# Attention over eight heads at a time: key and value windows of 128 columns, one buffer each

## The chip, the core and the metric

The kernel runs on one core of one Trainium2 chip. The core has five engines that run their own instruction streams and wait for each other by semaphores: TensorE (PE, with the loading of weights shown apart as PEld), VectorE (DVE), ScalarE (ACT), GpSimd (POOL) and SyncE (SP), which here issues nearly all the DMAs. The metric is the time of one launch on the device, in microseconds; lower is better. All arithmetic is done in 32 bits; a product is made of three TensorE passes over a high part and a low part of each operand.

## The reference

One transformer block on x of 2048 positions by 512 columns. A layer norm, then attention with 32 heads of 16 columns in which every position looks at 8 positions only: itself and the ones 2, 4, ... 14 before it. Then the output product and the residual; then a second layer norm and an MLP of width 1792 with a squared ReLU, again with a residual.

```python
qkv = transpose((layernorm(x) @ wqkv).reshape(B, S, 3, H, Dh))   # H = 32, Dh = 16
idx = pos[:, None] - arange(8)[None, :] * 2                      # positions before 0 are masked
logits = einsum("bhsd,bhswd->bhsw", q, k[idx]) * Dh ** -0.5
o = einsum("bhsw,bhswd->bhsd", softmax(logits), v[idx])
h = x + o @ wo
r = max(layernorm(h) @ w1 + b1, 0)
out = h + (r * r) @ w2 + b2
```

## The kernel before, in words

The 16 row tiles of 128 positions are taken in a permuted order, so that the positions a head looks at lie in one partition. The work has these stages. First the queries, keys and values of the first four tiles, one fourth of the columns at a time (products of 384 columns, `qkv`); then those of the other twelve tiles (`first_phase`, products of 512 columns). Each result leaves PSUM by ScalarE (`evac`) and goes to a scratch tensor in DRAM, `qkv_d`, laid out by groups of `GC` columns (`store`). After that come three rounds `u` of the MLP on four tiles each, with two products per slot, `mlp1` (line 228) and `mlp2` (line 900), and a last round with fewer multiplications (`products_a`, `products_b`, line 823).

Attention runs on VectorE and GpSimd beside these products, from about 25 us on. It is a Python generator, `attention()`. It goes over items: an item is a stretch `s` of 2 positions per partition, and `ng` groups of `GH` heads (`G` = 8 groups of 4 heads, `GC` = 64 columns). For each group of an item there is

- a load of a window of keys (`load_k`) and one of values (`load_v`) from `qkv_d` into SBUF, and for two groups together one of queries (`load_q`), all issued on SP; ScalarE copies the queries to PSUM (`q_to_psum`, line 268);
- on VectorE `dots` (line 340: queries times keys, 1024 elements a partition, into a tile `pr`), a reduction over the 16 columns of a head (line 374), and one item later `weigh` (line 351: weights times values, again into a `pr`);
- on GpSimd `add_up` (line 408), three halving additions over the window into `o`.

The softmax between (lines 363 to 393, and an exponential on ScalarE, line 397) is done for a whole item at once. The tiles `k` and `v` have two buffers each, `pr` has three for both uses.

The order of instructions on each engine is fixed when the program is built. `end_slot(pe)` closes a slot of TensorE's work; it adds the slot's planned length to `now["pe"]`, runs the chores that were put down for the slot, and calls `pump()`, which takes steps from the generator until the planned time of VectorE, `now["dve"]`, has reached that of TensorE. Each `yield` names the planned cost of a step; `SLOW` multiplies it. `o_T` and `o_split` call `pump(until=s)`, which takes steps until a stretch's `o` is complete. Each engine then executes its list in order; SP too, so a load that waits for its buffer holds up the DMAs behind it.

Scratch rows of 2 KB (`row()`, a pool of `ROWS` = 15 buffers) serve many names: `xt`, `xh`, `xl`, `h`, `hn`, `oh`, `ol`, `r`, `rl`. The high part `rh` of the hidden rows has a pool of its own, of four.

VectorE also makes what TensorE waits for: the low parts `xl` and `ol` of transposed operands (line 155), the residual `h` (line 666), the low parts of the MLP's input in `big_l`.

Of the kernel before, what the change touches and what calls it, by code (L numbers as in the profile page):

```python
# [16 lines left out]
P = 128  # L17
# [5 lines left out]
G = 8  # L23
# [6 lines left out]
ROWS = 15  # L30
LAG = 3
HALF = 2.6
# [26 lines left out]
def block_kernel(ctx, tc, x, wqkv, wo, w1, b1, w2, b2, out):  # L59
# [196 lines left out]
    def load_q(n, j):  # L256
        s, g0, ng = items[n]
        u, b, e, i0 = where(s)
        q = att.tile([P, 2, RI, GC], F32, name="q")
        nc.sync.dma_start(q.rearrange("p j i c -> p j (i c)"),  # L260
                          chain(e, g0 + j, 0, PAD + CH // 2 * b + i0,
                                [[R * GC, P], [CS, 2], [1, RI * GC]]))
        return q

    def q_to_psum(q):
        qp = psum.tile([P, D], F32, name="qp", tag="qp")[:, :2 * RI * GC].rearrange(
            "p (j i c) -> p j i c", j=2, i=RI)
        nc.scalar.copy(qp, q)  # L268
        return qp

    def attention():
# [3 lines left out]
        def ready(n):  # L275
            gps = [(items[n][1] + j) // 2 for j in range(0, items[n][2], 2)] if n < N else []
# [13 lines left out]
        def load_k(n, j):  # L290
            if ready(n) and (n, j) not in ks:
                ks[n, j] = ks[n - 1, j] if items[n][0] == 1 else load_window(n, j, 1, "k")
                if j % 2 == 0:
                    qs[n, j] = load_q(n, j)
# [11 lines left out]
        for j in range(2):  # L306
            load_k(0, j)
        for j in range(2):
            load_v(0, j)
        for _ in range(DELAY):  # L310
            yield None
        for n in range(N + 1):
# [5 lines left out]
            if new:  # L318
# [3 lines left out]
                for j in range(2):  # L322
                    load_k(n, j)
# [11 lines left out]
            def dots(j):  # L335
                kwin = window(ks[n, j], s, [1, GC])
                pr = att.tile([P, RI, W, GH, DH], F32, name="pr", bufs=3)
                if j % 2 == 0:
                    qps["now"] = qps.pop((n, j))
                nc.vector.tensor_tensor(  # L340
                    out=pr.rearrange("p i w h d -> p i w (h d)"),
                    in0=qps["now"][:, j % 2].unsqueeze(2).to_broadcast([P, RI, W, GC]),
                    in1=kwin, op=ALU.mult)
                load_k(*ahead(n, j, 2))
                return pr

            def weigh(j):
                load_v(n - 1, j)
                vwin = window(vs[n - 1, j], s1, [DH, GH], [1, DH])
                p2 = att.tile([P, RI, W, GH, DH], F32, name="pr", bufs=3)  # L350
# [5 lines left out]
                load_v(*ahead(n - 1, j, 2))  # L356

            for j in range(max(ng, ng1)):
                if j < ng:
                    pr = dots(j)  # L360
                    yield 1.22
                if old and j == 0:
                    nc.vector.tensor_reduce(out=sm, in_=e1.rearrange("p i w h -> p i h w"),
                                            axis=X, op=ALU.add)
                    yield 0.23 + 0.035 * ng1
                if 0 < j < ng1 or 0 < j == ng1 < ng:
                    if j == 1:
                        nc.vector.tensor_tensor(
                            out=e1, in0=e1, op=ALU.mult,
# [889 lines left out]
```

## Time and profile before

| what | us |
|---|---|
| median of 3 runs (504.65 to 506.39) | 505.88 |
| the profiled execution, first to last instruction | 501.7 |
| TensorE busy | 496.2 (99%) |
| weight loads busy | 421.2 (84%) |
| VectorE busy | 382.9 (76%) |
| ScalarE busy | 298.3 (59%) |
| GpSimd busy | 356.2 (71%) |
| share of TensorE in the chain that ended last | 98% |
| data moved by DMA | 102.61 MB, mean 205 GB/s |

The span is the profiled execution from its first to its last instruction; the times of the runs lie about 4 us above it, since a run also holds what is before and after. TensorE's busy time has to be read with care, as its instructions overlap in the records; how often a new one starts says more. The granted clock of TensorE was 1.000 throughout.

### The profile page before, as it was taken

What the parts mean: (1) busy time and instruction counts of PE and PEld (TensorE: products, weight loads), DVE (VectorE), ACT (ScalarE), POOL (GpSimd) and SP (SyncE); (2) the same over time, 40 slices, a digit from 0 to 9 for tenths busy, and PEclk for the clock granted to TensorE, in tenths of its full rate; (3) what the DMA queues carried; (4) which work ended last, traced back from release to release, by engine and by line L of the source; (5) the groups of instructions that cost most, each with busy time, mean ns of one, the idle gap of its engine ahead of it and who ended that gap; (6) DMA issues with size and microseconds to landing.
All of it is one profiled execution on the core that took longest, in us unless ns stands there. A gap on an engine that the chain in (4) does not pass through costs nothing.

```text
span 501.7 us, 7533 instructions
## 1 busy us (share of the span) xinstructions
PE 496.2 (99%) x2422; PEld 421.2 (84%) x2422; DVE 382.9 (76%) x520; ACT 298.3 (59%) x538; POOL 356.2 (71%) x434
## 2 busy tenths in 40 slices
PE   8999999999999999999999999999999999999997
PEld 7999888888888888888888888888888888998986
DVE  6479899988989989788879998888975147833223
ACT  4635777668346758378564555755555837666551
POOL 5714898886685999969777877769799464775610
PEclk9999999999999999999999999999999999999999
DMA  9668979989698989679577756967665472354112
GB/s 275 202 205 243 300 237 312 270 273 275 212 223 256 299 277 260 205 216 237 190 254 209 215 146 192 237 209 242 210 159 115 112 197 84 137 161 143 64 43 84
DMA packets 109359, 102.61 MB, mean 205 GB/s; under 512 B 29448, under 2 KB 77832, under 8 KB 109320
## 3 DMA queue, kind: packets, MB, share of 16 engines
q1 hardware_dynamic: 108376, 101.61, 69.5%
q10 hardware_dynamic: 944, 0.52, 0.3%
q8 instruction: 19, 0.31, 0.3%
q14 instruction: 20, 0.16, 0.1%
HBM read 72.65 MB, written 24.25 MB: 193 GB/s over the span
## 4 chain that ended last, share of the span: by engine, by line
PE 98%; DMA 1%; ACT 0%; ACTq 0%; DVE 0%; issue 0%
PE mm L228 49%; PE acc L900 30%; PE wo L228 9%; PE mm L823 7%; PE tr L201 2%; DMA wraw<-in_A_wqkv_dram 1%; PE half L923 0%; ACTq L562 0%; ACT big_h L152 0%; ACT xh L152 0%; PE tr L730 0%; DVE h L925 0%
## 5 line engine op out<-in xcount | busy, mean ns | idle before, releaser
L408 POOL TENSOR_TENSOR pr<-pr 128x512 f32<-128x512 f32 (+1 forms) x128 | 133.9, 1046 | 35.1 <-DVE pr L351 29.7
L228 PE MATMUL mm<-big_l,w_h 128*128 128x512 f32 x336 | 88.4, 389 | 0.0
L351 DVE TENSOR_TENSOR pr<-ex,v 128x1024 f32<-128x1024 f32 x64 | 78.0, 1220 | 12.7 <-POOL o L408 9.8
L340 DVE TENSOR_TENSOR pr<-qp,k 128x1024 f32<-128x1024 f32 x64 | 76.8, 1200 | 11.1 <-ACT qp L268 7.6
L374 DVE TENSOR_REDUCE ex<-pr 128x64 f32<-128x1024 f32 x64 | 78.5, 1226 | 2.0
L228 PEld LDWEIGHTS mm<-big_l,w_h 128*128 128x128 f32 x336 | 63.0, 188 | 13.2 <-issue 0.2
L155 POOL TENSOR_TENSOR rl<-r,rh 128x512 fp32r<-128x512 f32 x42 | 55.2, 1317 | 22.3 <-ACT rh L152 22.2
L228 PE MATMUL mm<-big_l,xh 128*128 128x512 f32 (+1 forms) x208 | 55.8, 378 | 0.0
L228 PE MATMUL mm<-big_h,xh 128*128 128x512 f32 (+1 forms) x208 | 53.6, 379 | 0.8 <-ACT xh L152 0.8
L228 PE MATMUL mm<-big_h,xl 128*128 128x512 f32 (+1 forms) x208 | 52.7, 375 | 0.0
L900 PE MATMUL acc<-big_l,rh 128*128 128x512 f32 x190 | 52.2, 390 | 0.0
L900 PE MATMUL acc<-big_h,rh 128*128 128x512 f32 x190 | 52.1, 391 | 0.0
L900 PE MATMUL acc<-big_h,rl 128*128 128x512 f32 x190 | 51.7, 389 | 0.0
L228 PE MATMUL mm<-big_l,w_l 128*128 128x512 f32 x168 | 44.9, 389 | 0.0
L228 PEld LDWEIGHTS mm<-big_h,xh 128*128 128x128 f32 x208 | 37.7, 188 | 7.7 <-ACT xh L152 1.9
L228 PEld LDWEIGHTS mm<-big_h,xl 128*128 128x128 f32 x208 | 38.2, 188 | 6.1 <-DVE xl L155 0.3
L900 PEld LDWEIGHTS acc<-big_h,rl 128*128 128x128 f32 x190 | 35.7, 188 | 7.4
L900 PEld LDWEIGHTS acc<-big_l,rh 128*128 128x128 f32 x190 | 35.5, 188 | 7.4
L228 PEld LDWEIGHTS mm<-big_l,xh 128*128 128x128 f32 x208 | 37.5, 188 | 4.9
L900 PEld LDWEIGHTS acc<-big_h,rh 128*128 128x128 f32 x190 | 34.9, 188 | 6.7
L876 ACT ACTIVATE r<-mm,b_sb 128x512 f32<-128x512 f32 x42 | 28.8, 685 | 18.9 <-PE mm L228 18.1
L228 PEld LDWEIGHTS mm<-big_l,w_l 128*128 128x128 f32 x168 | 31.5, 188 | 6.6
(163 smaller groups left out, 912.3 us busy)
## 6 DMA issues: line engine op xcount, KB each, us to landing
k<-qkv_d SPq DMA_DIRECT2D x48, 288.0 KB, 3.5
v<-qkv_d SPq DMA_DIRECT2D x48, 288.0 KB, 3.9
qkv_d<-y SPq DMA_DIRECT2D x18, 512.0 KB, 4.1
big_l<-w2l_d SPq DMA_DIRECT2D x24, 256.0 KB, 2.6
xt<-in_A_x_dram SPq DMA_DIRECT2D x16, 256.0 KB, 4.1
q<-qkv_d SPq DMA_DIRECT2D x32, 128.0 KB, 3.1
h<-in_A_x_dram SPq DMA_DIRECT2D x16, 256.0 KB, 3.8
h_d<-h SPq DMA_DIRECT2D x16, 256.0 KB, 2.5
```

Source lines behind the costliest of these rows:

```text
L155: eng.tensor_tensor(out=dst, in0=src, in1=h, op=ALU.subtract)
L201: nc.tensor.transpose(tr[:, k, :], src[:, k * P:(k + 1) * P], ident)
L228: nc.tensor.matmul(ps, l(k), r(k), start=(n == 0), stop=(n == 3 * KB - 1))
L340: nc.vector.tensor_tensor(out=pr.rearrange("p i w h d -> p i w (h d)"), in0=qps["now"][:, j % 2].unsqueeze(2).to_broadcast([P, RI, W, GC]) ...
L351: nc.vector.tensor_tensor(out=p2, in1=vwin, op=ALU.mult, in0=e1[:, :, :, j * GH:(j + 1) * GH].unsqueeze(4).to_broadcast([P, RI, W, GH, DH]))
L374: nc.vector.tensor_reduce(out=lf[:, :, :, j * GH:(j + 1) * GH], in_=pr, axis=X, op=ALU.add)
L408: nc.gpsimd.tensor_tensor(out=dst, in0=p2[:, :, :w], in1=p2[:, :, w:2 * w], op=ALU.add)
L823: nc.tensor.matmul(ps, sta[y][:, k], mov[x][:, k], start=(first and q == 0), stop=(last and q == len(terms) - 1), skip_group_check=True)
L876: nc.scalar.activation(r, ps, AF.Relu, bias=b1_sb[:, f:f + 1])
L900: nc.tensor.matmul(acc[j], l[:, j * P:(j + 1) * P], w[f], start=(first and n < len(js)), stop=(last and n >= len(terms) - len(js)))
```

## The change

Groups become twice as wide and half as many: `G` = 4 groups of 8 heads, 128 columns. So every `dots`, its reduction and every `weigh` take 2048 elements a partition instead of 1024, and the product tile `pr` has 8 KB instead of 4 KB. An item holds the same heads as before, in 1 or 2 groups instead of 2 or 4. In detail:

- `k` and `v` windows are twice as large (4608 bytes a partition instead of 2304, and 5632 instead of 2816 in the first stretches) and have one buffer each. A load is asked for one group ahead instead of two.
- `pr` becomes two tiles of one buffer each: `pr0` for `dots`, `pr1` for `weigh`.
- Queries are loaded and copied to PSUM for one group at a time, which has the columns of two before: as many loads and copies as before.
- In the loop over an item's groups, `weigh(j)` now follows `dots(j)` at once, where before `weigh(j - 1)` did; the reciprocal moves to the sum before it.
- Stores to `qkv_d` have pieces of 1024 bytes instead of 512, and the stores of the first four tiles need one DMA instead of two.
- `rh` comes from the shared rows, of which there are 17 instead of 15 plus 4.
- The planner's costs are written anew; `pump()` stops 0.8 us (`LEAD`) before TensorE's planned time, and `HALF` grows from 2.6 to 4.6.
- Two normalisations and two transposes of `x` in the first stage come one slot earlier.
- Raw weights at the start, and the combined weights of the last round, find their place in the new `pr` tiles.

```diff
-G = 8
+G = 4
 GH = H // G
 GC = GH * DH
...
-ROWS = 15
+ROWS = 17
 LAG = 3
-HALF = 2.6
+HALF = 4.6
+LEAD = 0.8
...
-    items = [(s, g0, 2) for g0 in range(0, G, 2) for s in range(RI)]
-    items += [(s, g0, 4) for s in range(RI, NS) for g0 in range(0, G, 4)]
+    items = [(s, g0, 1) for g0 in range(G) for s in range(RI)]
+    items += [(s, g0, 2) for s in range(RI, NS) for g0 in range(0, G, 2)]
...
-        t = att.tile([P, R + W - 1, GC], F32, name=name)
+        t = att.tile([P, R + W - 1, GC], F32, name=name, bufs=1)
...
-        q = att.tile([P, 2, RI, GC], F32, name="q")
-        nc.sync.dma_start(q.rearrange("p j i c -> p j (i c)"),
+        q = att.tile([P, RI, GC], F32, name="q")
+        nc.sync.dma_start(q.rearrange("p i c -> p (i c)"),
                           chain(e, g0 + j, 0, PAD + CH // 2 * b + i0,
-                                [[R * GC, P], [CS, 2], [1, RI * GC]]))
+                                [[R * GC, P], [1, RI * GC]]))
...
             def dots(j):
                 kwin = window(ks[n, j], s, [1, GC])
-                pr = att.tile([P, RI, W, GH, DH], F32, name="pr", bufs=3)
-                if j % 2 == 0:
-                    qps["now"] = qps.pop((n, j))
+                pr = att.tile([P, RI, W, GH, DH], F32, name="pr", tag="pr0", bufs=1)
...
-                load_k(*ahead(n, j, 2))
+                load_k(*ahead(n, j, 1))
...
             def weigh(j):
                 load_v(n - 1, j)
                 vwin = window(vs[n - 1, j], s1, [DH, GH], [1, DH])
-                p2 = att.tile([P, RI, W, GH, DH], F32, name="pr", bufs=3)
+                p2 = att.tile([P, RI, W, GH, DH], F32, name="pr", tag="pr1", bufs=1)
...
-                load_v(*ahead(n - 1, j, 2))
+                load_v(*ahead(n - 1, j, 1))
 
             for j in range(max(ng, ng1)):
                 if j < ng:
                     pr = dots(j)
-                    yield 1.22
+                    yield 2.29
                 if old and j == 0:
                     nc.vector.tensor_reduce(out=sm, in_=e1.rearrange("p i w h -> p i h w"),
                                             axis=X, op=ALU.add)
-                    yield 0.23 + 0.035 * ng1
-                if 0 < j < ng1 or 0 < j == ng1 < ng:
-                    if j == 1:
-                        nc.vector.tensor_tensor(
-                            out=e1, in0=e1, op=ALU.mult,
-                            in1=sm.unsqueeze(2).to_broadcast([P, RI, W, ng1 * GH]))
-                    weigh(j - 1)
-                    yield 1.55 if j == 1 else 1.26
+                    nc.vector.reciprocal(sm, sm)
+                    yield 0.5 + 0.07 * ng1
+                    nc.vector.tensor_tensor(
+                        out=e1, in0=e1, op=ALU.mult,
+                        in1=sm.unsqueeze(2).to_broadcast([P, RI, W, ng1 * GH]))
+                if j < ng1:
+                    weigh(j)
+                    yield 2.63 if j == 0 else 2.33
...
-        while (done[until] < G) if until is not None else (now["dve"] < now["pe"]):
+        while (done[until] < G) if until is not None else (now["dve"] < now["pe"] - LEAD):
...
-            for j in range(2):
-                nc.sync.dma_start(chain(e, 2 * gp + j, 0, pos,
-                                        [[R * GC, P], [G * CS, 3], [1, RI * GC]]), y[:, :, j])
+            nc.sync.dma_start(chain(e, gp, 0, pos,
+                                    [[R * GC, P], [G * CS, 3], [1, RI * GC]]), y)
...
-        rh, rl = work.tile([P, D], F32R, name="rh", bufs=LAG + 1), row("rl", dt=F32R)
+        rh, rl = row("rh", dt=F32R), row("rl", dt=F32R)
...
-        if n in (11, 12):
-            at(0, x_norm, n - 7)
-        if n in (13, 14):
-            x_T(n - 9)
+        if n in (10, 11):
+            at(0, x_norm, n - 6)
+        if n in (12, 13):
+            x_T(n - 8)
```

The change moves instructions. First VectorE in the first round of the MLP, at the start of an item of 16 heads (`pr<-qp,k` is `dots`, `ex<-pr` its reduction, `pr<-ex,v` is `weigh`, `sm` and `ex,sm` are the softmax's scaling). Before:

```order
L340 TENSOR_TENSOR pr<-qp,k 128x1024
L363 TENSOR_REDUCE sm<-ex 128x32
L374 TENSOR_REDUCE ex<-pr 128x16x4
L380 RECIPROCAL sm<-sm 128x32
L340 TENSOR_TENSOR pr<-qp,k 128x1024
L368 TENSOR_TENSOR ex<-ex,sm 128x256
L351 TENSOR_TENSOR pr<-ex,v 128x1024
L374 TENSOR_REDUCE ex<-pr 128x16x4
```

And now, at the start of such an item:

```order
L335 TENSOR_TENSOR pr<-qp,k 128x2048
L358 TENSOR_REDUCE sm<-ex 128x32
L360 RECIPROCAL sm<-sm 128x32
L362 TENSOR_TENSOR ex<-ex,sm 128x256
L346 TENSOR_TENSOR pr<-ex,v 128x2048
L369 TENSOR_REDUCE ex<-pr 128x16x8
L335 TENSOR_TENSOR pr<-qp,k 128x2048
L346 TENSOR_TENSOR pr<-ex,v 128x2048
```

Between two `dots` there are now always a `weigh` and a reduction, and in the first pair of an item the three instructions of the softmax's scaling; the second load of keys into the one buffer falls into that stretch.

Next VectorE where the first stage of `first_phase` needs the low parts `xl` of the transposed tiles 6 and 7. Before:

```order
L340 TENSOR_TENSOR pr<-qp,k 128x1024
L368 TENSOR_TENSOR ex<-ex,sm 128x128
L351 TENSOR_TENSOR pr<-ex,v 128x1024
L374 TENSOR_REDUCE ex<-pr 128x16x4
L155 TENSOR_TENSOR xl<-tr,xh 128x512
L383 TENSOR_TENSOR ex<-ex,mask 128x128
L351 TENSOR_TENSOR pr<-ex,v 128x1024
L155 TENSOR_TENSOR xl<-tr,xh 128x512
```

And now:

```order
L335 TENSOR_TENSOR pr<-qp,k 128x2048
L358 TENSOR_REDUCE sm<-ex 128x16
L360 RECIPROCAL sm<-sm 128x16
L362 TENSOR_TENSOR ex<-ex,sm 128x128
L346 TENSOR_TENSOR pr<-ex,v 128x2048
L369 TENSOR_REDUCE ex<-pr 128x128
L156 TENSOR_TENSOR xl<-tr,xh 128x512
L374 TENSOR_TENSOR ex<-ex,mask 128x128
L379 TENSOR_REDUCE mx<-ex 128x16
L381 TENSOR_TENSOR ex<-ex,mx 128x128
L156 TENSOR_TENSOR xl<-tr,xh 128x512
```

In the program up to the first of these two `xl` there stand 8 `dots`, 8 reductions and 5 `weigh` before, and 4, 4 and 3 of double length now; the second `xl` no longer has a `weigh` in front of it.

Last TensorE, at the end of the stage with products of 384 columns, where the transposes of `x` stand a slot earlier. Before:

```order
L228 MATMUL mm<-big_l,xh 128x384 x4
L228 MATMUL mm<-big_h,xh 128x384 x4
L228 MATMUL mm<-big_l,xh 128x384 x4
L228 MATMUL mm<-big_h,xl 128x384 x4
L201 MATMUL tr<-ident,xt 128x128 x4
L228 MATMUL mm<-big_h,xh 128x384 x4
```

And now:

```order
L229 MATMUL mm<-big_l,xh 128x384 x4
L202 MATMUL tr<-ident,xt 128x128 x4
L229 MATMUL mm<-big_h,xh 128x384 x4
L229 MATMUL mm<-big_l,xh 128x384 x4
L229 MATMUL mm<-big_h,xl 128x384 x4
L202 MATMUL tr<-ident,xt 128x128 x4
```

One block of four transposes has moved ahead by one product. Otherwise TensorE's list has the same instructions in the same order as before.

More of the change, by code (lines that the diff above doesn't have):

```diff
@@ L275, in ready @@
         def ready(n):
-            gps = [(items[n][1] + j) // 2 for j in range(0, items[n][2], 2)] if n < N else []
+            gps = [items[n][1] + j for j in range(items[n][2])] if n < N else []
             return n < N and all((items[n][0] // RI, gp) in stored and gp in padded
@@ L511, in store @@
             elif c == 2:
[L512 removed]
+                stored.update((t // R, gp) for gp in range(G))
     ys = {}
```

61 lines of the change are left out of this document (27 added, 34 removed).

## The prediction

> **What bounds the kernel now.** I read the page first: span, busy times, and the chain that ended last.
>
> ```profile
> span 501.7 us, 7533 instructions
> PE 496.2 (99%) x2422; PEld 421.2 (84%) x2422; DVE 382.9 (76%) x520; ACT 298.3 (59%) x538; POOL 356.2 (71%) x434
> PE 98%; DMA 1%; ACT 0%; ACTq 0%; DVE 0%; issue 0%
> ```
>
> The chain runs through TensorE for 98% of the span. A busy TensorE can still be a waiting one, so next I asked for its waits in the whole trace, and for the busy times in windows of 20 us.
>
> ```profile
> PE tr L952 <- POOL ident masks.py:199: 1.3, 1, 1.3
> PE mm L228 <- ACT xh L152: 0.8, 1, 0.8
> ```
>
> ```profile
> 0.00:20.00 20.00, 17.87 (x96) 15.97 (x97) 13.29 (x21) 11.52 (x24) 14.29 (x27) 1.00 0.82 245
> 160.00:180.00 20.00, 20.00 (x89) 16.53 (x89) 18.26 (x22) 11.70 (x21) 17.29 (x17) 1.00 0.84 267
> 380.00:400.00 20.00, 20.00 (x90) 16.53 (x89) 5.70 (x9) 15.13 (x20) 13.10 (x18) 1.00 0.37 91
> ...
> 6.83 1.27 PE L228 MATMUL mm<-big_h,xh 128*128 128x384 f32 x4 [0.78 <-ACT xh L152]
> ```
>
> Two waits, 2.1 us together; the later one ends at 6.83, as the last row says. The columns are PE, PEld, DVE, ACT and POOL with instructions in brackets. TensorE does 89 products in 20 us while VectorE is busy for 18.26 us and GpSimd for 17.29, and 90 while VectorE is busy for 5.70. So its pace does not hang on how full the others are. The pieces of the chain say the same:
>
> ```profile
> 171.34 2.72 PE acc L900 x12
> 190.38 2.72 PE mm L228 x12
> ```
>
> Twelve products of 512 columns take 2.72 us, 227 ns each, in both kinds of product. TensorE issues without a gap from about 7 us to the end; what the other engines do is hidden unless it comes too late for TensorE.
>
> **The change, part by part.** TensorE's own list changes by one block of transposes that stands a slot earlier: **0**. All other terms are on engines under cover, so I price what they save, and then whether any of them gets later than TensorE allows. From the view that groups instructions by line and shape:
>
> ```profile
> L408 POOL TENSOR_TENSOR pr<-pr 128x512 f32<-128x512 f32 x64 | 83.8, 1309 | 30.1 <-DVE pr L351 29.7
> L374 DVE TENSOR_REDUCE ex<-pr 128x64 f32<-128x1024 f32 x64 | 78.5, 1226 | 2.0
> L351 DVE TENSOR_TENSOR pr<-ex,v 128x1024 f32<-128x1024 f32 x64 | 78.0, 1220 | 12.7 <-POOL o L408 9.8 <-POOL pr L408 0.6
> L340 DVE TENSOR_TENSOR pr<-qp,k 128x1024 f32<-128x1024 f32 x64 | 76.8, 1200 | 11.1 <-ACT qp L268 7.6 <-POOL o L408 3.4
> L408 POOL TENSOR_TENSOR pr<-pr 128x256 f32<-128x256 f32 x64 | 50.1, 783 | 5.0
> L408 POOL TENSOR_TENSOR o<-pr 128x128 f32<-128x128 f32 x64 | 30.1, 471 | 5.0
> L368 DVE TENSOR_TENSOR ex<-ex,sm 128x256 f32<-128x256 f32 x12 | 5.1, 421 | 0.0
> L391 DVE TENSOR_REDUCE mx<-ex 128x32 f32<-128x256 f32 x12 | 5.0, 413 | 0.0
> L268 ACT COPY qp<-q 128x256 f32<-128x256 f32 x32 | 12.0, 375 | 25.3 <-DMA q<-qkv_d 16.0 <-DVE pr L340 8.4 <-DVE ex L368 0.9
> ```
>
> *VectorE.* No row shows 2048 elements. Between 256 and 1024 a product grows by (1220 - 421) / 768 = 1.04 ns an element, a reduction by (1226 - 413) / 768 = 1.06. Another 1024 elements make 2.27 us for `dots`, 2.29 for `weigh`, 2.31 for the reduction: 6.87 us where two narrow groups took 7.29. Times 32 that is **13.5 us less work**. The bounds are no saving (twice the row) and 13.5; I take the second, since the slope is measured on the same operations.
>
> *GpSimd.* From 256 to 512 elements an addition grows by (1309 - 783) / 256 = 2.05 ns an element, so 1024 take 2.36 us (at most 2.62, twice the row). An `add_up` then is 2.36 + 1.31 + 0.78 = 4.45 us against 2 x 2.56 = 5.13: 32 times 0.68, **22 us less work**.
>
> Neither shows in the time, as nothing on the chain waited for them. And the planner does not leave the saving idle: it keeps VectorE level with TensorE's planned time, so attention runs ahead and ends earlier; the cover of the small urgent instructions does not grow by itself.
>
> *Where they could be late.* (1) **Keys and queries.** The next keys may be loaded only when `dots` has read the one buffer, and must be there when the next `dots` starts. Inside an item the scaling of the softmax, a `weigh` and a reduction lie between.
>
> ```profile
> L363 DVE TENSOR_REDUCE sm<-ex 128x32 f32<-128x256 f32 x12 | 4.9, 411 | 0.4 <-ACT ex L397 0.4
> 217.21 0.34 DVE L380 RECIPROCAL sm<-sm 128x32 f32<-128x32 f32 x1
> L247 SPq DMA_DIRECT2D k<-qkv_d x56: 319/320/843, 21.0 to 357.6; - x56
> k<-qkv_d SPq DMA_DIRECT2D x48, 288.0 KB, 3.5
> v<-qkv_d SPq DMA_DIRECT2D x48, 288.0 KB, 3.9
> q<-qkv_d SPq DMA_DIRECT2D x32, 128.0 KB, 3.1
> ```
>
> The window is 0.41 + 0.34 + 0.42 + 2.29 + 2.31 = 5.8 us. A load of 288 KB lands 3.5 us after its issue. The other 288 KB cost at least nothing and at most the same again (7.0). I take what moves 295 KB at the 267 GB/s of the window quoted: 1.1 us, so 4.6. Behind it the queries are issued some 0.4 us later (a key load holds SP 0.32 us, the median in the row), and ScalarE needs 0.38 us to copy them: 5.4 us. It fits by 0.4. Between items the maximum and the subtraction (0.4 us each) take the scaling's place, or stand beside it. (2) **Values**: from one `weigh` to the next of an item lie 2.31 + 2.27 = 4.6 us; a load lands after 3.9, or 5.0 with the 1.1: late by 0.4 in 12 places at most, where no chore fills the gap. (3) **GpSimd's sum** must have emptied `pr1` in the same 4.6 us: 4.45 fits, but one `rl` (1.3 us) ahead of it does not. VectorE waited 9.8 + 3.4 us for these sums and 7.6 for queries already; I put the new waits, 12 times 0.4 and about 12 times 1.2, against those 20.8 us and count **0** more. SP has 56 window loads to issue instead of 112.
>
> (4) **The rows.** `rh` now takes a third row per hidden block, so a row comes round sooner: 17 / 3 against 15 / 2 blocks, still beyond the three slots that `rh` and `rl` live. I count 0; a row that is freed late would hold ScalarE before `r`, and with it a bank that TensorE needs.
>
> (5) **Long instructions ahead of urgent ones.** The tightest places are these, where TensorE starts on a low part just after VectorE has written it:
>
> ```profile
> 60.86 1.23 DVE L374 TENSOR_REDUCE ex<-pr 128x64 f32<-128x1024 f32 x1
> 62.00 0.68 DVE L155 TENSOR_TENSOR xl<-tr,xh 128x512 fp32r<-128x512 f32 x1
> 62.73 1.19 PE L228 MATMUL mm<-big_h,xl 128*128 128x512 f32 x4
> ...
> 236.78 1.21 DVE L155 TENSOR_TENSOR ol<-pl,oh 128x512 fp32r<-128x512 f32 x1
> 238.50 1.07 PE L228 MATMUL wo<-wo_h,ol 128*128 128x512 f32 x4
> ```
>
> The `xl` ends at 62.68, 0.05 us before its use; the `ol` at 237.99, 0.51 before. Ahead of that `xl` there stand 21 attention instructions (8, 8 and 5) at 1.2 us, 25.5 us; now 11 (4, 4 and 3), 9.16 + 9.24 + 6.87 = 25.3. So it comes 0.2 us earlier, if VectorE waits no longer than the 1.7 us it waited before:
>
> ```profile
> 55.39 1.22 DVE L340 TENSOR_TENSOR pr<-qp,k 128x1024 f32<-128x1024 f32 x1 [1.68 <-POOL o L408]
> ```
>
> There the sum has 4.6 us plus some 1.9 of softmax, since an item is one group in that stage; 4.45 fits, and the wait should go. I count 0 to 2 us of gain in slack, nothing in time.
>
> (6) **The end of `o`.** ScalarE waited for the last sum of a stretch, and all it did later was late by that:
>
> ```profile
> 217.80 1.05 ACT L621 COPY pl<-o 128x1024 uint16<-128x1024 uint16 x1 [2.08 <-POOL o L408]
> ```
>
> Now `weigh` follows `dots` without the lag of a group, so `o` is whole earlier. A gain in slack again.
>
> The sum: 501.7 + 0 = 501.7 us, and the run's time lies 505.88 - 501.7 = 4.2 above the span: **505.9 us, no change**.
>
> **The rivals.** *A. The buffers bind* (slower). The place is the second `dots` of the 12 items with two groups, the price is how much keys, queries or the sum overrun their window. At 7.0 us for the keys the overrun is 2.0 us; at 1.0 it is 12 us over three rounds. VectorE can make up only where it idles for TensorE:
>
> ```profile
> 204.02 0.69 DVE L666 TENSOR_TENSOR h<-wo,h 128x512 f32<-128x512 f32 x1 [1.50 <-PE wo L228]
> 212.18 0.69 DVE L666 TENSOR_TENSOR h<-wo,h 128x512 f32<-128x512 f32 x1 [1.21 <-PE wo L228]
> ```
>
> With 2.7 us there and the 0.5 of slack before `ol` in each of three rounds, some 8 us would reach TensorE: 514. It decides from an overrun of about 0.35 us on. For it: VectorE is busy 18.26 of 20 us, and SP holds loads back behind others. Against: chores stand in many of the windows. [...]
>
> *B. An urgent instruction behind a long one* (slower). A miss at a place like the two of (5) costs up to one long instruction, 2.3 us, 1.2 on average; TensorE then is later against VectorE and the next places are safe. Two misses: 508.3. For it: slack of 0.05 and 0.51. Against: the counts above, and `LEAD`, which holds attention back by 0.8 us.
>
> *C. The rows bind* (slower): ScalarE held once per round for the 1.3 us of an `rl`: 3.9 us, 509.8. Against: the count in (4).
>
> *D. Faster.* TensorE may have room that its records hide, and the 13.5 us come through: 492. Against it stand 89 and 90 products in the two windows. Short of that, the start has 20.00 - 17.87 = 2.1 us of gaps, of which fewer and larger DMAs could win a part: 504.3. [...]
>
> **How the numbers follow.** Chances: forecast 0.60, A 0.13, B 0.19, C 0.04, D 0.04. A difference under 0.3% (1.5 us) cannot be told from none here. The forecast is no change; A, B and C are slower; D is faster: 0.04, 0.60, 0.36. The forecast's own range is 504.7 to 507.2, the spread of the runs and a stall of an us. The range for 8 in 10 reaches down to D's short form and takes in B and C and the cheaper half of A: 504.3 to 511.
>
> **What would show it.** Attention's last product of before:
>
> ```profile
> 378.84 1.23 DVE L351 TENSOR_TENSOR pr<-ex,v 128x1024 f32<-128x1024 f32 x1 [0.60 <-POOL pr L408]
> ```
>
> Right: TensorE's two waits stay the only ones; `dots` and `weigh` at 2.27 and 2.29 us, the wide sum at 2.4; attention ending earlier than these 380 us; no wait of ScalarE for `o` near 217 us. For A: waits of `dots` for `qp` or of `weigh` for a load or a sum, of over 0.4 us, in most items, followed by TensorE waiting for `ol` or for `big_l`. For B: one or two waits of TensorE for `xl` or `ol` of 1 to 2 us. For C: `r` or `rh` waiting on TensorE or GpSimd. The prediction is wrong if TensorE shows over 1.5 us of new waits, or a product takes other than 227 ns.

## The result, and the profile after

The changed kernel takes 526.38 us (median of 4 runs, 524.65 to 527.94), the kernel before 506.13 on the same chip. The ratio is 1.042, 95% interval 1.0395 to 1.0446: some 20 us slower, where no change was forecast and 511 was the end of the range. The profiled execution took 524.82 us, 1.8 us above its span. From the changed kernel's page:

```profile
span 523.0 us, 7203 instructions
PE 503.3 (96%) x2422; PEld 424.5 (81%) x2422; DVE 385.5 (74%) x424; ACT 299.0 (57%) x538; POOL 339.6 (65%) x338
PE 27%; DVE 4%; DMA 3%; ACT 2%; issue 2%; POOL 2%; SPq 0%; ACTq 0%; POOLq 0%; DVEq 0%
```

The chain that ended last is no longer TensorE's alone. Its waits in the whole trace (us in total, times, longest), which were two of 2.1 us together:

```profile
PE mm L229 <- DVE big_l L156: 8.2, 2, 5.1
PE tr L202 <- ACT hn L197: 2.1, 1, 2.1
PE tr L202 <- DVE ol L156: 1.6, 1, 1.6
PE wo L229 <- DVE ol L156: 1.5, 2, 1.0
PE tr L944 <- POOL ident masks.py:199: 1.3, 1, 1.3
PE mm L229 <- ACT xh L153: 0.7, 1, 0.7
PE tr L718 <- ACT hn L197: 0.6, 1, 0.6
```

The windows of 20 us show a second loss. After the TensorE columns the granted clock is the number behind POOL's:

```profile
160.00:180.00 20.00, 14.58 (x56) 11.61 (x56) 17.31 (x18) 11.33 (x25) 10.06 (x8) 0.83 0.61 209
260.00:280.00 20.00, 18.14 (x68) 14.80 (x69) 17.77 (x20) 8.65 (x15) 10.69 (x8) 0.83 0.50 169
```

56 products where there were 89, and a clock of 0.83 where it was 1.00. TensorE's list is almost the same in both kernels, so I set the start of each product beside its start before. It gets late in these places only (`y` is a result on its way to DRAM, `hn` the normalised `h`):

| start in the changed kernel (us) | late against before, from then on (us) | what TensorE waited for |
|---|---|---|
| 124.85, transposes of `x` | 1.5 | VectorE's `ol` |
| 160.41, transposes of `hn` | 2.0 | ScalarE's `y` |
| 167.56, first product of the MLP | 7.3, and 9.5 some 5 us later | VectorE's `big_l`; then products at half speed |
| 248.46, output product | 10.0 | VectorE's `ol` |
| 261.86, second round of the MLP | 13.4, and 16.2 some 6 us later | VectorE's `big_l`; then products at half speed |
| 343.88, output product | 17.4 | VectorE's `ol` |
| 354.46, transposes of `hn` | 19.8 | ScalarE's `hn` |
| 440.54 and 448.38, last round | 20.6, 21.2 | `hn`, `wo_l` |

**The long waits.** What VectorE, GpSimd and TensorE did at the first of them, from the timelines of the three engines:

```profile
160.69 6.06 DVE L156 TENSOR_TENSOR big_l<-pl,big_l 128x256 fp32r<-128x256 f32 x4 [1.74 <-ACT big_l L153]
...
160.41 3.79 POOL L396 TENSOR_TENSOR pr<-pr 128x1024 f32<-128x1024 f32 x2
164.29 0.78 POOL L396 TENSOR_TENSOR o<-pr 128x256 f32<-128x256 f32 x1
165.03 1.44 POOL L156 TENSOR_TENSOR big_l<-raw,big_h 128x512 fp32r<-128x512 f32 x1
...
161.36 1.09 PE L229 MATMUL mm<-big_h,xl 128*128 128x512 f32 x4
167.56 2.04 PE L229 MATMUL mm<-big_l,w_h 128*128 128x512 f32 x4 [5.11 <-DVE big_l L156]
169.40 1.91 PE L229 MATMUL mm<-big_l,w_l 128*128 128x512 f32 x4
```

Four subtractions of 256 columns, the low parts of the MLP's input, take 6.06 us, while GpSimd goes through a sum and one subtraction of its own. And behind the wait four products of 512 columns take 1.91 us, 427 ns from one to the next instead of 227. Before the change the same four took 2.94 us, and the product behind them came without a wait:

```profile
155.64 2.94 DVE L155 TENSOR_TENSOR big_l<-pl,big_l 128x256 fp32r<-128x256 f32 x4 [0.65 <-ACT big_l L152]
158.50 0.74 DVE L155 TENSOR_TENSOR big_l<-tr,big_l 128x256 fp32r<-128x256 f32 x2
...
160.28 1.09 PE L228 MATMUL mm<-big_l,w_h 128*128 128x512 f32 x4
```

The form of the operand tells why. `pl` lies in SBUF (a tile turned by DMA), `tr` in PSUM (turned by TensorE). In the groups by line and shape, of before:

```profile
L155 DVE TENSOR_TENSOR big_l<-pl,big_l 128x256 fp32r<-128x256 f32 x16 | 10.2, 694 | 2.8 <-ACT big_l L152 2.8
L155 DVE TENSOR_TENSOR big_l<-tr,big_l 128x256 fp32r<-128x256 f32 x14 | 5.2, 412 | 1.1 <-PE acc L900 0.9 <-ACT big_l L152 0.2
```

and of the changed kernel, with the rows of attention itself:

```profile
L156 DVE TENSOR_TENSOR big_l<-pl,big_l 128x256 fp32r<-128x256 f32 x16 | 17.7, 1165 | 4.8 <-ACT big_l L153 4.8
L156 DVE TENSOR_TENSOR big_l<-tr,big_l 128x256 fp32r<-128x256 f32 x14 | 5.0, 408 | 0.0
L335 DVE TENSOR_TENSOR pr<-qp,k 128x2048 f32<-128x2048 f32 x32 | 73.1, 2284 | 16.2 <-ACT qp L269 13.6 <-DMA v<-qkv_d 1.8
L346 DVE TENSOR_TENSOR pr<-ex,v 128x2048 f32<-128x2048 f32 x32 | 73.3, 2289 | 11.9 <-POOL o L396 9.7 <-DMA v<-qkv_d 0.5
L369 DVE TENSOR_REDUCE ex<-pr 128x128 f32<-128x2048 f32 x32 | 73.2, 2287 | 0.6
L396 POOL TENSOR_TENSOR pr<-pr 128x1024 f32<-128x1024 f32 x32 | 77.9, 2435 | 24.9 <-DVE pr L346 24.9
L396 POOL TENSOR_TENSOR pr<-pr 128x512 f32<-128x512 f32 x32 | 42.5, 1327 | 2.5
L396 POOL TENSOR_TENSOR o<-pr 128x256 f32<-128x256 f32 x32 | 23.8, 743 | 2.5
```

The same subtraction takes 412 ns with one operand in PSUM, and 694 and now 1165 ns in the mean with both in SBUF. Theory **P**: such a subtraction is held until GpSimd's running instruction ends, and the next one by GpSimd's next instruction (the four at 160.69 us end at 163.08, 164.49, 165.35 and 166.75, each 0.28 us after an instruction of GpSimd), so a sum with an addition of 2.4 us in it holds four in a row for 6 us.

**The short waits.** Theory **Queue**: a load of keys or values into its buffer stands at the head of SP's in-order queue until VectorE has read the buffer, and what stands behind (queries, the transposes by DMA) comes late. SP's waits at the loads, before:

```profile
SPq L247 <- DVE pr L351: 45.6, 33, 3.5
SPq L247 <- DVE pr L340: 38.9, 23, 3.6
SPq L247 <- DVE mx L391: 22.3, 12, 2.9
SPq L247 <- DVE sm L363: 16.6, 10, 3.0
SPq L247 <- DVE ex L368: 16.5, 10, 2.6
```

and now:

```profile
SPq L248 <- DVE pr L346: 59.6, 25, 5.9
SPq L248 <- DVE sm L358: 46.2, 12, 6.5
SPq L248 <- DVE pr L335: 44.4, 12, 7.0
```

In the sum it is little more, 150 against 140 us; but 49 pieces of up to 7.0 us have taken the place of 88 of up to 3.6. Followed back in the trace, the wait of TensorE at 124.85 leads to a load of queries behind a load of keys: `dots` waited 1.4 us for them, and the `ol` that TensorE needed stood behind it. The waits at 343.88 and 354.46 lead to a transpose of `o` that SP issued at 332.7, behind such a load (330.96) and another transpose. On the way from there, the `ol` stood behind a late `dots` of 2.3 us (340.94), and the `hn` waited for a normalisation that stood in GpSimd's list behind the sum of a late `weigh` and an `rl`, until 352.2 us. The wait at 248.46 fits P: its `ol<-pl,oh` took 2.13 us beside an addition, the one at 343.14 only 0.68.

### The profile page after: what moved, and what is told of

Its sections match the earlier page's. It is cut to its first block, busy times and chain, and to the rows that moved or that the text cites. A ratio compares the mean times of both kernels' runs of the same rounds, so it can differ in the third digit from the quotient of the medians.

```text
span 523.0 us, 7203 instructions
## 1 busy us (share of the span) xinstructions
PE 503.3 (96%) x2422; PEld 424.5 (81%) x2422; DVE 385.5 (74%) x424; ACT 299.0 (57%) x538; POOL 339.6 (65%) x338
## 5 line engine op out<-in xcount | busy, mean ns | idle before, releaser
L396 POOL TENSOR_TENSOR pr<-pr 128x1024 f32<-128x1024 f32 x64 | 120.4, 1881 | 27.5 <-DVE pr L346 24.9
L229 PE MATMUL mm<-big_l,w_h 128*128 128x512 f32 x336 | 92.0, 401 | 8.2 <-DVE big_l L156 8.2
L335 DVE TENSOR_TENSOR pr<-qp,k 128x2048 f32<-128x2048 f32 x32 | 73.1, 2284 | 16.2 <-ACT qp L269 13.6
L229 PEld LDWEIGHTS mm<-big_l,w_h 128*128 128x128 f32 x336 | 65.4, 195 | 22.8 <-issue 9.0
L346 DVE TENSOR_TENSOR pr<-ex,v 128x2048 f32<-128x2048 f32 x32 | 73.3, 2289 | 11.9 <-POOL o L396 9.7
L369 DVE TENSOR_REDUCE ex<-pr 128x128 f32<-128x2048 f32 x32 | 73.2, 2287 | 0.6
L229 PE MATMUL mm<-big_l,w_l 128*128 128x512 f32 x168 | 46.6, 400 | 0.0
L229 PEld LDWEIGHTS mm<-big_l,w_l 128*128 128x128 f32 x168 | 32.7, 195 | 7.0
```

What stands on the lines that cost most here:

```text
L229: nc.tensor.matmul(ps, l(k), r(k), start=(n == 0), stop=(n == 3 * KB - 1))
L335: nc.vector.tensor_tensor(out=pr.rearrange("p i w h d -> p i w (h d)"), in0=qps.pop((n, j)).unsqueeze(2).to_broadcast([P, RI, W, GC]), in1 ...
L346: nc.vector.tensor_tensor(out=p2, in1=vwin, op=ALU.mult, in0=e1[:, :, :, j * GH:(j + 1) * GH].unsqueeze(4).to_broadcast([P, RI, W, GH, DH]))
L369: nc.vector.tensor_reduce(out=lf[:, :, :, j * GH:(j + 1) * GH], in_=pr, axis=X, op=ALU.add)
L396: nc.gpsimd.tensor_tensor(out=dst, in0=p2[:, :, :w], in1=p2[:, :, w:2 * w], op=ALU.add)
```

## Experiments

All times are medians; the kernel before ran beside each set on the same chip (504.2 to 505.2 us). The ratio is against it, with its 95% interval in brackets. The theories besides P and Queue are **R** (long sums in GpSimd's queue delay the normalisation of `h`, as they do on the way to the wait at 354.46), **B** or **Data** (one buffer makes the keys come too late), **Plan** (the planner's settings).

### Low parts from PSUM

```diff
-        lo_T(tr, hs_, ls_)
+        for d, h in zip(ls_, hs_):
+            lo(nc.vector, d, bank[0][:, D // 2:].rearrange("p (k c) -> p k c", k=2), h)
...
```

> The changed kernel, but the low parts of the h tiles turned by DMA (`big_l<-pl,big_l`, two of 256 columns a tile) take their first operand from a spare half bank of PSUM (a constant) instead of the turned tile in SBUF. The count of VectorE's instructions and their sizes stay; what is left out is that these low parts have the right values. Theory P (VectorE's subtractions with all operands in SBUF are held until GpSimd's running addition ends, and hold a PSUM bank that TensorE needs; the wait then drops the clock): these instructions go from 0.4 to 2.6 us each to 0.41 us, the waits of TensorE at 162 us (5.3) and 258 us (3.3) fall to under 1 us, the granted clock is 1.00 in both windows, and the time falls by 11 to 13 us: 513 to 516. Theory R (the h tiles come late because their normalisation stands behind a sum in GpSimd's queue): the subtractions get short, but TensorE waits as long, 523 to 526. Theory B (one buffer each for keys and values makes attention late): 526, no change.

514.06 us (512.11 to 515.83), 1.018 [1.0135, 1.0225]. VectorE and GpSimd at the same place, from the timelines:

```profile
164.67 1.42 DVE L156 TENSOR_TENSOR big_l<-qp,big_l 128x256 fp32r<-128x256 f32 x4 [1.73 <-ACT big_l L153]
...
164.40 3.78 POOL L400 TENSOR_TENSOR pr<-pr 128x1024 f32<-128x1024 f32 x2
```

Four subtractions in 1.42 us beside the same sum that held them for 6.06. TensorE's wait there is 0.6 us, its clock 1.00 throughout. P is shown for 12 us of the 20, with the size that was expected; at this place R is worth at most the 0.6 us that stay.

### Two buffers, and where the load stands

The rows of the first MLP weight overlap in SBUF to make room.

```diff
-        t = att.tile([P, R + W - 1, GC], F32, name=name, bufs=1)
+        t = att.tile([P, R + W - 1, GC], F32, name=name, bufs=2)
```

> The changed kernel with two buffers each for keys and values, loaded one group ahead, so no load waits for a product to finish. Room is made by letting the rows of the first MLP weight overlap by 512 columns in SBUF: all instructions stay, the MLP's values are wrong. Theory B in full (the single buffers make attention late and everything behind it): `dots` no longer waits for queries, TensorE's nine waits fall to the two of before, 506 to 508. Theory P + B in part (the single buffers cause only the waits at 123, 342 and 352 us, 1.8 + 1.1 + 2.3 = 5.2 us; the larger ones come from subtractions held by GpSimd): 520 to 522. Theory P alone: 526.

512.77 us (512.32 to 518.88), 1.0161 [1.0129, 1.0194]: a larger gain than P + B in part had it. The execution profiled was the longest of the five; both long waits were in it (5.1 and 3.5 us), and the short ones at 123, 342 and 352 us were gone. A second profile of the same kernel was to tell what the shorter executions lack.

> The kernel with two buffers, one group ahead, once more, for a profile of another execution: one of about 512.5 us should lack one of the two waits for held subtractions (5.3 us at the first round of the MLP, 3.6 us at the second) and its stretch at the lower clock; if it has both and other waits are missing, the two causes hang together in another way than thought.

513.27 us; the execution profiled took 513.87. TensorE's longest wait, and SP's waits for VectorE at the loads that are over 1 us:

```profile
PE mm L229 <- DVE big_l L156: 5.1, 1, 5.1
```

```profile
SPq L248 <- DVE sm L358: 6.8, 2, 6.5
SPq L248 <- DVE pr L346: 4.7, 5, 2.2
```

As expected, one of the two long waits is missing, that of the second round. The program is the same in both executions; what differs is when the four subtractions start. In the slower one the second starts at 255.03 us, inside an addition that began at 254.79, and takes 2.61 us. In this one three of them are done in 0.42 us each before the sum begins at 255.09. So some 5 of this kernel's 13 us hang on a microsecond or two between VectorE and GpSimd; the execution with both long waits gains 7.5 us (518.88). The times of the other executions, 512.3 to 513.8, fit one long wait, but no profile shows them. The next run separates the second buffer from the free queue.

```diff
-                load_k(*ahead(n, j, 1))
+                load_k(*ahead(n, j, 2))
...
-                load_v(*ahead(n - 1, j, 1))
+                load_v(*ahead(n - 1, j, 2))
```

Not shown above: two windows instead of one are loaded at the start, and a window that two items share is not asked for before its first item has it.

> Two buffers each for keys and values as in the run with two buffers, but each load now goes out two groups ahead into the buffer that the running product reads, as before the change: it stands at the head of SP's queue until that product ends, though its data are never late. Theory Queue (what costs is that SP stands still behind such a load, and the queries and the DMA transposes behind it come late): as with one buffer, 520 to 527, waits at 123, 342 and 352 us back. Theory Data (what costs is that keys or queries arrive after the product could start): as with two buffers one group ahead, 511 to 515.

528.41 us (525.35 to 530.61), 1.0477 [1.0422, 1.0532]: all of the gain is gone. SP's waits at the loads are long again; the first row of them:

```profile
SPq L248 <- DVE pr L349: 48.4, 21, 8.6
```

In the three rows of this kind they come to 129 us, where two buffers loaded one group ahead had some 14. The waits of TensorE at the output product and the transposes of `hn` are back with 1.0 and 2.1 us (at 345 and 356 us); those for `big_l` are 5.1 and 1.6 us. The one at 123 us is not back; in its place there are two, of 2.1 and 2.9 us at 62 and 69 us, which were not followed back. A second buffer alone buys nothing, then: two buffers whose loads stand at SP's head cost as much as one.

### Both causes, and what the edits bring along

The two edits together, with the low parts of the `o` tiles from PSUM too:

```diff
-        (at if n or t >= 12 else midway)(n, lo_T, tr, [oT[t][0]], [oT[t][1]])
+        (at if n or t >= 12 else midway)(n, o_low, oT[t])
...
```

> Both edits together, and the low parts of the o tiles turned by DMA (`ol<-pl,oh`, `ohl<-pl,ohl`) take their first operand from PSUM too. If P and B together are the whole cause: 506 to 509, with TensorE's waits under 3 us in all and no window with a granted clock under 1.00. If something else holds (planner, rows of the ring): above 512.

506.65 us (506.33 to 507.88), 1.0041 [1.0027, 1.0055]; the clock is 1.00 in every window of 20 us. TensorE's waits come to 4.8 us, not under 3: 2.7 us more than before, none longer than 0.8 but for the very first. What brings these was not followed up.

> Only what the edits brought along: the overlapping rows of the first MLP weight, and the one bank of PSUM held for all queries with a spare half; one buffer each and the low parts as in the changed kernel. It leaves the MLP's values wrong and nothing else. Every theory: as the changed kernel, 524 to 528. Below 520 the edits themselves would be a part of the gain seen.

```diff
+            bank.append(psum.tile([P, D], F32, name="qp", tag="qp"))
+            nc.scalar.copy(bank[0][:, D // 2:], ident.unsqueeze(1).to_broadcast([P, 2, P]))
...
```

525.68 us (524.11 to 526.99), 1.0419: what the edits bring along does nothing. Between this run and the one with both edits lie 19.0 us: P and Queue are nearly the whole loss. Alone the two edits gain 12 and 13 us, together more than 19, since with two buffers one of the long waits mostly fell away too.

### The planner's settings

```diff
-HALF = 4.6
-LEAD = 0.8
+HALF = 2.6
+LEAD = 0.0
```

> The changed kernel with the planner's two settings of before (`HALF = 2.6`, `LEAD = 0`): only the order of attention against the other work moves, by up to one long instruction. Theory Plan (the settings cause the loss): 506 to 510. Theory P + B (any order has collisions as long as sums and products are long): 518 to 534, with other places of TensorE's waits.

526.41 us, 1.0417 [1.0381, 1.0453]. The places move (new waits of 2.9 us at 213 us, and of 0.6 and 0.9 at 307 and 316), the sum doesn't. Plan falls.

### Shorter additions, fewer such subtractions

```diff
-            nc.gpsimd.tensor_tensor(out=dst, in0=p2[:, :, :w], in1=p2[:, :, w:2 * w], op=ALU.add)
+            for h in range(max(w // 2, 1)):
+                sl = slice(2 * h, 2 * h + 2) if w > 1 else slice(0, 1)
+                nc.gpsimd.tensor_tensor(out=dst[:, :, sl], in0=p2[:, :, sl],
+                                        in1=p2[:, :, w + sl.start:w + sl.stop], op=ALU.add)
```

> The changed kernel with the first addition of a sum (1024 columns, 2.4 us) split in two of 512 (1.3 us each). Theory Length (a subtraction is held for the longest GpSimd instruction, so it is the length of the single addition that counts): the longest hold falls from 2.6 to 1.5 us, but four subtractions in a row are held by four additions in turn, so 520 to 524. Theory Place (it counts that a sum of 4.6 us runs when the four subtractions come, however it is cut): 524 to 528, with the same two waits of 5 and 3 us.

522.47 us (522.12 to 525.53), 1.037 [1.0335, 1.0405]. The first long wait is 4.0 us instead of 5.1, the second is gone: Length and Place both count, and the gain is what Length gave.

```diff
-HV = (0,1,4,5,8,9,12,13)
+HV = (8,9,12,13)
```

> The changed kernel, complete, but the four h tiles 0, 1, 4 and 5 are turned by TensorE instead of DMA, so their low parts are made from PSUM: 16 transposes more for TensorE (1.8 us). Theory P: the waits at 162 and 258 us fall to under 1 us without any wrong value; 526 - 12.8 + 1.8 = 515 (512 to 518). Theory R or B: 526 to 528.

521.66 us (521.26 to 523.61), 1.0348 [1.032, 1.0376], not 515. The long waits for `big_l` are gone (0.7 and 0.4 us left), but TensorE waits elsewhere, 2.2 us for ScalarE's `oh` and 2.1 for its `r` among them, and the clock is down to 0.83 in the 10 us after the latter. So turning tiles on TensorE takes P away and brings waits for ScalarE that my sum did not have; I did not look for their cause.

### Later loads with one buffer

```diff
-                load_k(*ahead(n, j, 1))
                 return pr
...
-                load_v(*ahead(n - 1, j, 1))
...
                 if j < ng1:
                     weigh(j)
+                    if j < ng:
+                        load_k(*ahead(n, j, 1))
                     yield 2.63 if j == 0 else 2.33
+                elif j < ng:
+                    load_k(*ahead(n, j, 1))
                 if j < ng:
                     nc.vector.tensor_reduce(out=lf[:, :, :, j * GH:(j + 1) * GH], in_=pr, axis=X,
                                             op=ALU.add)
+                    if j < ng1:
+                        load_v(*ahead(n - 1, j, 1))
```

> The changed kernel, complete, with one buffer each, but each load of keys is written into the program after the next `weigh` and each load of values after the next reduction, so that by the plan the product that frees the buffer has ended when SP comes to the load, and SP does not stand behind it. Theory Queue: as with two buffers one group ahead, 511 to 518; SP's waits for VectorE at the loads fall from 150 us to under 50. Theory Data (a load of 4 us cannot fit between two products with one buffer): 524 to 530, `dots` waits for queries more than the 13.6 us it does now.

522.12 us (520.88 to 523.85), 1.0343 [1.0317, 1.0368]: 4 us gained, not 8 to 15. SP's waits at the loads fell from 150 to 89 us only, where under 50 was expected; their first row:

```profile
SPq L248 <- DVE pr L345: 40.2, 19, 5.8
```

So VectorE is often later than planned when SP comes to a load; why was not looked into. `dots` waited 12.5 us for queries (13.6 before this edit), so Data is not borne out either.

> The same with the low parts of all tiles turned by DMA made from PSUM (their values are wrong): the two mechanisms P and Queue taken away together, with one buffer each and no overlap of the weight's rows. If these two are the whole cause: 505.5 to 509, as with two buffers. If a single buffer costs something of its own: 511 or more.

The diff is the one above with the two on low parts. 509.59 us (508.86 to 509.96), 1.0095 [1.0078, 1.0112], between the two answers. One buffer with later loads stays 3 us above two buffers one group ahead; with SP still held for as long as in the run before, this is no proof that the buffer costs something of its own.

> The later loads and the first addition of each sum split in two, a complete kernel. If both savings add up (Queue: 8 to 13 us, Length: 3.9 us): 510 to 515. If the stalls that remain are the same ones for both: as e9. It would beat the kernel before only below 503, which neither theory gives.

518.6 us (517.9 to 520.65), 1.0277 [1.0252, 1.0303], with both diffs above: 7.8 us against 4.3 and 3.9, so they add up. The time is still outside the 510 to 515 expected, because that counted 8 to 13 us for the later loads. The long waits stay, with 4.0 and 2.5 us.

### The clock

```diff
+        for n in range((40, 24, 0)[u]):
+            nc.tensor.matmul(bank[0][:, D // 2:], wo_h[:, n % KB, :P], wo_h[:, n % KB, :D // 2],
+                             start=True, stop=True)
```

> The changed kernel with products that nobody reads put on TensorE just where it waits for held subtractions: 40 of 256 columns (4.8 us) ahead of the MLP's first round, 24 (2.9 us) ahead of the second, into the spare half bank of PSUM. Theory Clock (the granted clock falls after such a wait, and the next 10 to 12 products take 427 ns instead of 227): the waits are filled, the next products take 227 ns, 526.4 - 2.0 - 2.9 = 521.5 (520 to 524). If the lower clock has nothing to do with the wait: 526 to 528.

521.4 us (520.01 to 522.59), 1.0317 [1.029, 1.0345], as Clock gave. TensorE's timeline with the wait filled:

```profile
165.64 4.95 PE L1101 MATMUL qp<-wo_h 128*128 128x256 f32 x40
170.42 1.09 PE L229 MATMUL mm<-big_l,w_h 128*128 128x512 f32 x4
171.35 1.07 PE L229 MATMUL mm<-big_l,w_l 128*128 128x512 f32 x4
```

TensorE does some 7.8 us of useless work, and the kernel is 5 us faster: the products behind start 227 ns apart again. (In the execution profiled the clock fell at two other waits, of 2.7 and 2.1 us, which ended at 126.77 and 351.40 us; it is 0.83 in the 10 us from 120.)

### P mended in a complete kernel

```diff
         lo_T(tr, hs_, ls_)
+        gate[:] = [ls_[1][:, 1, P - 1:].bitcast(F32)]
...
+            if todo and gate:
+                g = small.tile([P, 1], F32, name="gate")
+                nc.gpsimd.tensor_tensor(out=g, in0=gate.pop(), in1=mhalf, op=ALU.mult)
             for a in todo:
                 add_up(*a)
```

> The changed kernel, complete, with one instruction more on GpSimd per round of the MLP: ahead of the first sum that follows the low parts of the turned h tiles in the program it reads one number of these low parts, so this sum starts only when the four subtractions are done. Theory P: the subtractions take 0.41 us again, TensorE's two waits fall to under 1 us with no product of 427 ns after them, and the time is that of the run with low parts from PSUM, 512 to 516. If the sums that now come 2 to 3 us later make attention late: 517 to 526.

516.93 us (514.8 to 518.06), 1.0232 [1.0206, 1.0259]; the median lies between the two answers. From the timelines of VectorE and GpSimd:

```profile
161.70 1.43 DVE L156 TENSOR_TENSOR big_l<-pl,big_l 128x256 fp32r<-128x256 f32 x4 [1.74 <-ACT big_l L153]
...
163.21 0.19 POOL L412 TENSOR_TENSOR gate<-big_l,mhalf 128x1 f32<-128x1 f32 x1 [1.75 <-DVE big_l L156]
163.36 3.77 POOL L396 TENSOR_TENSOR pr<-pr 128x1024 f32<-128x1024 f32 x2
```

GpSimd idles for 1.75 us, the subtractions take 1.43 us from SBUF, TensorE's wait behind them is 0.6 us. One small instruction per round, which only changes what runs beside what, wins 9.5 us. That settles P in a complete kernel.

> The gate and the later loads together, complete, one buffer each. P and Queue: 508 to 512, as with low parts from PSUM and later loads (509.6). If the two mends disturb each other: above 514. Not under 503 by either, so not faster than the kernel before.

510.54 us (509.74 to 513.83), 1.0123 [1.0088, 1.0158]: both mends in one complete kernel, one buffer each, 16 us of the 20. From its page:

```profile
PE 497.8 (98%) x2422; PEld 420.5 (83%) x2422; DVE 377.0 (74%) x424; ACT 297.7 (59%) x538; POOL 341.0 (67%) x341
```

None of the runs is faster than the kernel before, and nothing here says that one could be: there TensorE waits for 2.1 us in all.

## Why the prediction was wrong

**What bounds.** Right: TensorE, which before the change waited for only 2.1 us; and so every loss starts with a new wait of TensorE. The 4.2 us between span and run were not what they were taken for: they set a median of runs beside the span of one execution. A run lies 1.7 to 2.2 us above its own span (524.82 to 523.0, 504.23 to 502.1).

**The work saved.** Right. `dots`, reduction and `weigh` take 2.28, 2.29 and 2.29 us (forecast 2.27, 2.31, 2.29); in the groups attention's three rows went from 233.3 to 219.6 us, 13.7 less (13.5). The wide addition takes 2.44 us (2.36), a sum 4.51 (4.45), and GpSimd saved 19.8 us (22). As said, none of it shows in the time. The page does not even show it in VectorE's busy time (385.5 us, before 382.9): an instruction that is held counts as busy, `big_l<-pl,big_l` alone with 7.5 us more.

**(1) Keys and queries.** The sizes were right: a load of keys lands in 4.0 us (4.6), one of values in 4.5 (5.0). The waits were not: `dots` waited 13.6 us for queries where it had waited 7.6, and 0 more was counted. The step that failed is the sentence that SP has 56 loads to issue instead of 112, which counted the queue as relieved. What grew is the length of one hold at SP's head, 3.6 to 7.0 us, and what stands behind it was not asked: 1.8 + 1.2 + 2.4 us on TensorE. Rival A had the place near (queries, then `ol` late) but priced data that arrive late. The run with two buffers loaded two groups ahead shows that data asked for early do not help while SP stands still for them.

A second buffer is worth what the place of its loads makes of it: two buffers gained 13 us where the load could go out without waiting (512.8; 7.5 us in the execution with both long waits), nothing where it went out behind the running product (528.4).

**(2) Values, (3) the sum.** Right: `weigh` waited 0.5 us for values, and VectorE's waits for the sums fell from 13.8 to 9.7 us.

**(4) The rows.** Right for the time: ScalarE once waited 4.8 us before `r` for a row that goes to DRAM, and TensorE was not held behind it.

**(5) Long instructions ahead of urgent ones.** Here is the step that failed most. I counted what stands ahead of an urgent instruction on its own engine and took its own length as fixed. At the `xl` (operand in PSUM) the count held: TensorE has no wait there. At the four `big_l` and at the `ol` of the example, now 2.13 us long, it did not, as their length depends on GpSimd. The rows to see it were in the profile of before, one even in the prediction: `ol<-pl,oh` with 1.21 us beside `xl<-tr,xh` of the same shape with 0.68, and the groups of `big_l` with 694 and 412 ns above. I took the 1.21 for its length. (Four `dots` at 2.27 us are 9.08, not 9.16; it changes nothing.) Nor were the low parts at the start of a round among my tight places. Rival B named urgent low parts, with 1.2 us a miss: the waits at 124.85 and 343.88, 1.6 and 1.0 us, are of its kind and size. The two long waits were 5.1 and 3.1 us, and with each the granted clock fell to 0.50 for 6.83 us.

What I had not weighed is what runs beside such a subtraction: beside a sum of GpSimd it takes 0.36 us with one operand in PSUM (the run with low parts from PSUM) and 1.5 with both in SBUF (the changed kernel). Seen so, the change was a risk, since it nearly doubles GpSimd's longest addition (1.31 to 2.44 us).

**(6) The end of `o`.** Right: ScalarE's wait for a sum near 217 us is gone. By the clock attention ends later (its last product starts at 384.29 us, before at 378.84), against TensorE's program some 14 us earlier, as TensorE is 19.8 us late there.

**The price of a wait.** My rivals counted a wait of TensorE at its length. All its waits are 16.6 us, 14.5 more than before; the two long ones cost 2.2 and 2.9 us more through the clock, 5 of the 21 us, and the run with filler products won 5.0 of them back. So both signs that the prediction had named for being wrong came true: more than 1.5 us of new waits, and products of 427 ns.

## What to carry to other kernels

When an instruction under cover gets longer, ask three things beside its own cost: which instructions of other engines are held beside it (here VectorE's subtractions with both operands in SBUF, 1.5 us in the mean beside a sum of GpSimd instead of 0.41), what stands behind its transfers in an in-order queue, and whether a wait that it causes on TensorE can drop the clock (in the changed kernel waits of 5.1 and 3.1 us did, one of 2.1 us did not). The clue is one shape with two mean durations in the groups of the profile: look at what differs in its operands and at what ran beside the long ones. Issue a load into a buffer only where, in the order of the queue, the buffer is already free, or give it a second buffer so that it can go out at once (here later loads gained 4 us, two buffers 13).

## What was not expected of the hardware

Subtractions and GpSimd's instructions take turns: the hold does not end with the instruction that began it. In the changed kernel the four at 160.69 us took 2.4, 1.5, 0.9 and 1.5 us. In the split kernel four subtractions of 0.41 us in a row were held by four GpSimd instructions in turn and took 1.3, 1.5, 1.5 and 0.9 us, so shorter additions won little there (5.0 us in all instead of 6.1).

Whether a wait drops the clock is not a matter of its length alone. In the kernel with filler products a wait of 2.69 us was followed by products of half speed; TensorE's timeline and two windows of 3.41 us:

```profile
126.77 1.08 PE L202 MATMUL tr<-ident,xt 128*128 128x128 f32 x4 [2.69 <-DVE ol L156]
127.51 2.05 PE L229 MATMUL wo<-wo_h,oh 128*128 128x512 f32 x4
```

```profile
123.02:126.43 3.41, 1.06 (x5) 0.56 (x3) 3.28 (x4) 3.41 (x8) 2.45 (x4) 1.00 0.81 277
126.43:129.84 3.41, 3.07 (x10) 2.61 (x11) 3.32 (x4) 1.35 (x3) 3.33 (x3) 0.50 0.85 182
```

The half clock begins at 126.43, before the wait ends, and lasts for the 3.41 us of the second window; in the first TensorE had waited 2.35 us. In the split kernel a longer wait at the same place was followed by products at full speed, with a granted clock of 1.00 in the 10 us from 125:

```profile
127.16 0.63 PE L202 MATMUL tr<-ident,xt 128*128 128x128 f32 x4 [2.96 <-DVE ol L156]
127.54 1.17 PE L229 MATMUL wo<-wo_h,oh 128*128 128x512 f32 x4
```

In the changed kernel the half clock begins at 165.40 and 260.98 us, again before the two long waits end (167.56 and 261.86), and lasts 6.83 us each time; products then start 427 ns apart instead of 227. In the 3.41 us before, TensorE had waited 2.95 and 2.22 us. In the same execution waits of 1.60 and 2.10 us, which ended at 124.85 and 354.46, left the clock at 1.00, and so did one of 2.6 us for `ol` in the run with low parts from PSUM. No run shows what decides between a wait of 2.69 us that drops the clock and one of 2.96 that does not.
